# Weight pieces prepared only in the up stages, stored at once from six buffers; sums of the first down projection taken earlier, seven operand pairs

## The chip, the cores and the metric

The kernel runs on one core of one Trainium2 chip. The metric is device time in microseconds (us), the median of three runs. A core has TensorE (PE, matrix products), ScalarE (ACT), VectorE (DVE), GpSimd (POOL) and SyncE (SP). SP computes nothing; it issues transfers. POOL here issues the stores of activations.

## The reference

Attention in two steps through 32 packed queries, a gated MLP, and a second MLP with h·cos(h):

```python
p_packed = sm_attn(p, k, v)                 # 8 batches, 8 heads, 576 tokens, head size 64
out = sm_attn(q, p_packed, p_packed)
x = out.transpose(0, 2, 1, 3).reshape(4608, 512)
g = x @ w_gate                              # 512 -> 1536
x = (g / (1 + exp(-g)) * (x @ w_val)) @ w_out     # 1536 -> 512
h = x @ w_in                                # 512 -> 2048
out = (h * cos(h)) @ w_out2                 # 2048 -> 512
```

The weights arrive as 64-bit floats.

## The kernel before

Products are made in three passes of two-part operands: each operand is split into a high part (ACT copies it with rounding) and a low part (DVE subtracts), and PE multiplies high by high, high by low, low by high. That is the helper `split` (lines 85 to 87).

The work has three stages, one after the other on PE.

*Up stages, one for each batch 0 to 7* (`a_up`, lines 429 to 479). A batch has 24 slots: 12 column blocks f of the gated MLP, two token halves c. In a slot PE makes two groups of six matmuls of 288 columns (`pg` and `pv`, line 462), ACT takes the silu of the one (line 470), DVE multiplies by the other (line 471), and after the second half POOL stores the pair to DRAM as `h1` (line 478). A table `sched` hangs further steps on the end of a slot: the scores of later batches, loads of keys, queries and values, and `w2_step`. Batch 0 makes its weights with `a_wp0` (lines 400 to 412), later batches with `a_wp`.

*First down projection* (loop at lines 770 to 806, product in `strassen`, line 549). The tokens are taken in five sets, four with 512 columns to a product and one with 256. Each set is a two-by-two scheme with seven products, in the order 0, 4, 6, 1, 3, 2, 5. A product is 36 matmuls in two halves m. `prep` splits the operands of the next product, three pairs `g` to a product; for products 1 and 5 it first makes differences of the loaded activations `hr` (lines 519 to 523). The weights of the seven products are in `w1u`, the results go to `x2d`.

*Second MLP* (lines 819 to 980), fed from `w2u` and `w2d` in DRAM.

What links the stages is the preparation of weights. 88 pieces of 128x256 are loaded as 64-bit words (`raw`), decoded by two ACT and two DVE operations (`w2t`, `w2f`, lines 97 to 110), for the first 56 pieces combined into Strassen sums (`w2c`, line 346), split (`w2p`) and stored to `w1u` (42 stores), `w2u` (56) and `w2d` (32, for the last 32 pieces, which need no sums). `w2_step` (lines 387 to 396) does this in halves: an even step stores what is ready, loads the piece two ahead, does up to two pending splits and decodes one piece; an odd step does one pending split. There are 16 steps in each of batches 1 to 6, 24 in batch 7, and 56 in the first four sets of the down projection, two to a product.

The order on each engine is the order of the code. Engines wait for each other by semaphores, and an engine that waits holds up all that is behind it. SP has one queue, in which loads and stores follow each other.

Of the kernel before, what the change touches and what calls it, by code (L numbers as in the profile page):

```python
# [10 lines left out]
F32 = mybir.dt.float32  # L11
# [21 lines left out]
NG = NPF // 2  # L33
ATT = 26
ORDER = (0, 4, 6, 1, 3, 2, 5)
# [9 lines left out]
def attention_mlp_kernel(ctx: ExitStack, tc: tile.TileContext, qT, kT, vP, pP, wgv, w12, out):  # L45
# [4 lines left out]
    st = ctx.enter_context(tc.tile_pool(name="st", bufs=4))  # L50
    stage = {n: ExitStack() for n in ("dc", "ups", "att", "gates", "da", "db", "dw")}

# [3 lines left out]

    dc, att = pool("dc"), pool("att")
    gw, ups = pool("gates", "right"), pool("ups", "right")
# [262 lines left out]

    w2_raw, w2_f, w2_todo, w2_done = {}, {}, [], []
    NITEM = 2 * NW1 + 4 * NF2

    def w2_load(i):
        if i < NITEM:
            r = w2_raw[i] = dc.tile([128, 256, 2], U32, tag="r", name="raw", bufs=3)
            SP.dma_start(
                out=r, in_=w12[i // 2, :, 256 * (i % 2):256 * (i % 2) + 256].bitcast(U32).rearrange(
                    "p (n t) -> p n t", t=2)  # L330
            )

    def w2_small(name):
        return dc.tile([128, 256], F32, tag="s", name=name, bufs=10)
# [44 lines left out]

    def w2_store():  # L380
        while w2_done:
            p, dst = w2_done.pop(0)
            SP.dma_start(out=dst, in_=p.bitcast(F32))

    w2_n = [0]

    def w2_step():
        s_ = w2_n[0]
        w2_n[0] += 1
        if s_ % 2 == 0 and s_ // 2 < NITEM:  # L390
            w2_store()
# [36 lines left out]

    def a_up(b, sched):
        def side(k):  # L430
# [3 lines left out]
        for f in range(NF1):  # L434
# [8 lines left out]
            if b == 0:  # L443
                for u in range(2):
                    for c in range(2):
                        for o, p_ in zip((0, 128), banks[c]):
                            PE.matmul(
                                out=p_, lhsT=w[:, u, o:o + 128], rhs=a2[0, u][:, HS * c:HS * c + HS],
                                start=(u == 0), stop=(u == 1),
                            )  # L450
                    if u == (f == 0) and f + 1 < NF1:
                        a_wp0(f + 1)
            for c in range(2):
                sl = slice(HS * c, HS * c + HS)
                pg, pv = banks[c]
                for o, p_ in ((0, pg), (128, pv)):
                    n = 0
                    for u in range(2):
                        if b == 0:
                            continue  # L460
                        for (x, y) in PASSES:
                            PE.matmul(  # L462
                                out=p_, lhsT=w[u][:, x, o:o + 128], rhs=a2[b, u][:, y, sl],
                                start=(n == 0), stop=(n == 5),
                            )
                            n += 1
                if b == 0 and f > 0:
                    u_step(2, 1)
                s_ = ups.tile([128, HS], F32, tag="silu", name="silu", bufs=4)
                ACT.activation(out=s_, in_=pg, func=AF.Silu)  # L470
                DVE.tensor_tensor(out=h_[:, sl], in0=s_, in1=pv, op=ALU.mult)  # L471
                if b == 0:
                    u_step(0, 1)
                    u_step(1, 1)
                    if f == 0:
                        u_step(2, 1)
                if c == 1:
                    nc.gpsimd.dma_start(out=h1[f, :, S * b:S * b + S], in_=h_)
                side(2 * f + c)

# [25 lines left out]
    def new_g(N):  # L506
        n = g_n[0] % 5
        g_n[0] += 1
        return late["da" if n < 2 else "db"].tile(
            [128, 2, 2, N], F32R, tag="g", name="g", bufs=2 if n < 2 else 3  # L510
        )

    def prep(s_, n, fp):
        if s_ >= len(SETS):
            return
        N = SETS[s_][1]
        x11, x21, x22, x12 = (raw1.get((s_, k, t, fp)) for k, t in ((0, 0), (1, 0), (1, 1), (0, 1)))
# [6 lines left out]
        src = {0: x11, 4: x21, 6: x22, 1: x22, 3: x11, 2: x12, 5: x21}[n]  # L524
        g = g1[n, fp] = new_g(N)
        split(src, g[:, 0], g[:, 1])

# [102 lines left out]
    with tc.manual_schedule():  # L630
# [87 lines left out]
        for b in range(B):  # L718
# [14 lines left out]
            else:  # L733
# [18 lines left out]
            a_up(b, sched)  # L752
            w2_store()

# [12 lines left out]
        def nxt(s_, i):  # L767
            return (s_, ORDER[i + 1]) if i < 6 else (s_ + 1, ORDER[0])

        for s_ in range(len(SETS)):  # L770
            end = s_ == len(SETS) - 1
            for i in range(7):
                evict0 = strassen(s_, i, 0)
                if not end:
                    w2_step()
                prep(*nxt(s_, i), 0)
# [3 lines left out]
                prep(*nxt(s_, i), 2)  # L780
                if i == 3:
                    load_h(s_ + 1, 0, 0)
                elif i == 4:
                    load_h(s_ + 1, 1, 0)
                elif i == 5:
                    load_h(s_ + 1, 1, 1)
                    load_h(s_ + 1, 0, 1)
                if not end:
                    w2_step()
                elif i == 4:  # L790
                    w2_store()
# [4 lines left out]
                elif i == 5:  # L796
# [4 lines left out]
                elif i == 6:  # L801
                    sums_x2(2)
# [4 lines left out]

        for n in ("db", "da", "dc"):
            stage[n].close()
# [211 lines left out]
```

## Time and profile before

| | us |
|---|---|
| median of 3 runs (lowest, highest) | 1645.67 (1644.96, 1646.34) |
| the profiled execution | 1643.67 |
| its span in the profile | 1641.8 |
| PE busy in it | 1508.0 (92%) |
| DVE busy, ACT busy | 1123.9 (68%), 866.2 (53%) |
| mean granted TensorE clock | 0.961 of full |

The span starts with the first instruction and ends with the last; 1.9 us of the profiled execution lie around it. PE is busy for 92% on average, but the second of the page's views, which cuts the span in 40 slices, shows nine tenths or more in each of the last 18 and less in most of those before. The three stages therefore have to be read apart.

### The profile page before, as it was taken

The numbers are of one execution on the slowest core, as the hardware profiler recorded it, in microseconds if no ns is written. First come the engines' busy times: TensorE is split into PE (matmuls) and PEld (weight loads), VectorE is DVE, ScalarE is ACT, GpSimd is POOL, SyncE is SP. The second block draws the span as 40 slices with busy tenths as digits, with TensorE's granted clock in tenths as the row PEclk, the third lists the DMA queues.
The fourth block names the chain that finished last, engine by engine and source line by source line (L and its number), as shares of the span: only waits on it lengthen the run. The fifth ranks groups of instructions, "written<-read, shape, count | busy, mean of one in ns | idle before, by whom it ended". The sixth has DMA issues, their size and how long they took to land.

```text
span 1641.8 us, 26374 instructions
## 1 busy us (share of the span) xinstructions
PE 1508.0 (92%) x9432; PEld 1287.0 (78%) x9432; DVE 1123.9 (68%) x2139; ACT 866.2 (53%) x1847; POOL 76.6 (5%) x158
## 2 busy tenths in 40 slices
PE   9898888889978588988888999999999999999999
PEld 6567777777867366767767899999999999999997
DVE  6756776777856377666768777677667667667564
ACT  5755645646645144534535655655656556555552
POOL 0001111111110000001000000000000000000000
PEclk9989999999989788989889999999999999999999
DMA  9926557655488744635615866656666666666641
GB/s 339 331 95 224 204 186 250 210 186 209 166 280 288 287 124 171 202 129 174 219 59 209 321 190 223 205 201 227 198 215 209 202 218 200 217 204 202 194 145 64
DMA packets 160626, 335.72 MB, mean 204 GB/s; under 512 B 16880, under 2 KB 35312, under 8 KB 160496
## 3 DMA queue, kind: packets, MB, share of 16 engines
q1 hardware_dynamic: 149872, 296.28, 54.0%
q0 software_dynamic: 10624, 37.76, 5.9%
q8 instruction: 75, 1.23, 0.3%
q14 instruction: 55, 0.45, 0.1%
HBM read 252.71 MB, written 81.26 MB: 203 GB/s over the span
## 4 chain that ended last, share of the span: by engine, by line
PE 52%; DVE 7%; DMA 4%; ACT 3%; issue 2%; SPq 0%; ACTq 0%; DVEq 0%
PE acc L884 24%; PE p L869 21%; PE o L549 7%; ACT g L86 2%; DMA raw<-in_w 1%; DMA w<-w1u 1%; DVE g L87 1%; DVE hr L520 1%; DVE hr L521 1%; DVE hr L519 1%; DVE hr L523 1%; DMA w2d<-w2p 1%; DVE x2e L569 0%; DMA hr<-h 0%; DVE xs L87 0%
## 5 line engine op out<-in xcount | busy, mean ns | idle before, releaser
L884 PE MATMUL acc<-wd,g 128*128 128x512 f32 x1728 | 418.1, 391 | 0.0
L869 PE MATMUL p<-xs,up 128*128 128x384 f32 x2016 | 379.2, 339 | 2.1 <-DMA up<-w2u 1.4
L884 PEld LDWEIGHTS acc<-wd,g 128*128 128x128 f32 x1728 | 323.0, 188 | 61.4
L869 PEld LDWEIGHTS p<-xs,up 128*128 128x128 f32 x2016 | 359.0, 188 | 14.0 <-DMA up<-w2u 1.4
L549 PE MATMUL o<-g,w 128*128 128x512 f32 (+1 forms) x1260 | 294.4, 393 | 65.3 <-ACT g L86 45.3
L549 PEld LDWEIGHTS o<-g,w 128*128 128x128 f32 x1260 | 232.2, 201 | 127.2 <-ACT g L86 52.0
L462 PE MATMUL pg<-a,wp 128*128 128x288 f32 x1008 | 173.5, 309 | 36.7 <-ACT silu L470 28.2
L462 PEld LDWEIGHTS pg<-a,wp 128*128 128x128 f32 x1008 | 148.3, 196 | 60.9 <-ACT silu L470 30.3
L847 ACT ACTIVATE t<-c,quarter 128x384 f32<-128x384 f32 x144 | 88.6, 615 | 201.1 <-DVE c L957 195.3
L462 PE MATMUL pv<-a,wp 128*128 128x288 f32 x1008 | 167.1, 302 | 4.8 <-DVE h L471 3.0
L86 ACT ACTIVATE g<-hr 128x1024 fp32r<-128x1024 f32 (+1 forms) x105 | 98.8, 966 | 136.2 <-DVE hr L521 74.4
L87 DVE TENSOR_TENSOR g<-hr,g 128x1024 fp32r<-128x1024 f32 (+1 forms) x105 | 115.0, 1116 | 68.4 <-ACT g L86 67.9
L462 PEld LDWEIGHTS pv<-a,wp 128*128 128x128 f32 x1008 | 147.8, 194 | 7.6 <-DVE h L471 4.4
L471 DVE TENSOR_TENSOR h<-silu,pv 128x288 f32<-128x288 f32 x192 | 85.8, 447 | 51.5 <-PE pv L462 21.0
L470 ACT ACTIVATE silu<-pg 128x288 f32<-128x288 f32 x192 | 76.8, 410 | 67.2 <-PE pg L462 57.3
L857 DVE TENSOR_TENSOR g<-t,g 128x384 fp32r<-128x384 f32 x192 | 105.9, 551 | 8.0 <-ACT g L844 7.8
L952 DVE TENSOR_TENSOR u<-v,p 128x384 f32<-128x384 f32 x48 | 26.6, 554 | 119.4 <-PE p L869 119.0
L849 DVE TENSOR_TENSOR t<-t,k 128x384 f32<-128x384 f32 x192 | 106.0, 552 | 3.1 <-ACT k L853 1.5
L850 ACT ACTIVATE t<-t 128x384 f32<-128x384 f32 x192 | 98.1, 511 | 2.5 <-DVE t L849 2.4
L844 ACT ACTIVATE g<-t 128x384 fp32r<-128x384 f32 x192 | 98.7, 514 | 0.4 <-DVE t L855 0.4
L853 ACT ACTIVATE k<-t 128x384 int32<-128x384 f32 x192 | 98.1, 511 | 0.0
L898 DVE TENSOR_TENSOR oacc<-oacc,acc 128x512 f32<-128x512 f32 x108 | 73.8, 684 | 34.6 <-PE acc L884 34.6
(100 smaller groups left out, 1509.0 us busy)
## 6 DMA issues: line engine op xcount, KB each, us to landing
up<-w2u SPq DMA_DIRECT2D x336, 256.0 KB, 3.1
wd<-w2d SPq DMA_DIRECT2D x96, 512.0 KB, 6.2
h<-h POOLq DMA_DIRECT2D x96, 288.0 KB, 3.2
hr<-h SPq DMA_DIRECT2D x48, 512.0 KB, 7.2
raw<-in_w SPq DMA_DIRECT2D x88, 256.0 KB, 3.6
w2u<-w2p SPq DMA_DIRECT2D x56, 256.0 KB, 2.6
raw<-in_wgv SPq DMA_DIRECT2D x24, 512.0 KB, 8.6
w1u<-w2p SPq DMA_DIRECT2D x42, 256.0 KB, 2.4
```

The lines of the kernel that those rows point to most:

```text
L86: ACT.activation(out=hi, in_=src, func=AF.Copy)
L87: eng.tensor_tensor(out=lo, in0=src, in1=hi.bitcast(F32), op=ALU.subtract)
L462: PE.matmul(out=p_, lhsT=w[u][:, x, o:o + 128], rhs=a2[b, u][:, y, sl], start=(n == 0), stop=(n == 5),)
L549: PE.matmul(out=acc, lhsT=wd1[n, fp][:, j, 256 * x + 128 * m:256 * x + 128 * m + 128], rhs=g1[n, fp][:, y, j, :], start=(first and q == 0) ...
L844: ACT.activation(out=three["g"][:, 0, :], in_=three["t"], func=AF.Copy)
L847: ACT.activation(out=now["t"], in_=now["h"], func=AF.Identity, scale=1.0 / TWO_PI, bias=quarter)
L849: DVE.tensor_tensor(out=one_["t"], in0=one_["t"], in1=one_["k"], op=ALU.subtract)
L850: ACT.activation(out=one_["t"], in_=one_["t"], func=AF.Sin, scale=SIN_SCALE)
L853: ACT.activation(out=now["k"], in_=now["t"], func=AF.Copy)
L857: DVE.tensor_tensor(out=three["g"][:, 1, :], in0=three["t"], in1=three["g"][:, 0, :].bitcast(F32), op=ALU.subtract)
L869: PE.matmul(out=out, lhsT=w[:, u, 128 * k:128 * k + 128], rhs=x[:, v, k, :], start=(first and k == 0 and i == 0), stop=(last and k == 1 an ...
L884: PE.matmul(out=acc, lhsT=gs[p, a, t][:, x, o:o + 128], rhs=wd[j, f][:, y, :], start=(f == 0 and n == 0), stop=(f == 3 and n == 2),)
```

## The change

`w2_step` now hangs on 22 of the 24 slots of batches 1 to 6 (all but 1 and 6) and twice on every slot of batch 7; none is left in the down projection. A split piece is stored by SP in the same step, where it was collected and stored at the next even step, and the split pieces have six buffers instead of three. The buffers lie in the pool of the up stages, which closes before the down projection; the attention pool has 24 buffers instead of 26. In batch 0 the weights of blocks 3 and 9 are made one block earlier.

In the down projection the differences leave `prep` for a table by product, `sums1`, which stands ahead of the splits; there are seven operand pairs instead of five, the loads for the next set are put at the products with numbers 4 and 5 in the order, and ten small matmuls (`keep_busy(10)`) stand ahead of the first product.

```diff
-ATT = 26
+ATT = 24
 def w2_put(w_, dst):
     def go():
-        p = dc.tile([128, 2, 256], F32R, tag="p", name="w2p", bufs=3)
+        p = ups.tile([128, 2, 256], F32R, tag="p", name="w2p", bufs=6)
         split(w_, p[:, 0, :], p[:, 1, :])
-        w2_done.append((p, dst))
+        SP.dma_start(out=dst, in_=p.bitcast(F32))
...
+        def packed(f):
+            if f < NF1 and f not in ahead:
+                ahead.add(f)
+                a_wp0(f)
...
+                    if f in early:
+                        packed(f + 2)
...
-        n = g_n[0] % 5
+        n = g_n[0] % 7
...
-        if n == 1:
-            DVE.tensor_tensor(out=x11, in0=x12, in1=x11, op=ALU.subtract)
-            DVE.tensor_tensor(out=x12, in0=x22, in1=x12, op=ALU.subtract)
-            DVE.tensor_tensor(out=x22, in0=x22, in1=x11, op=ALU.subtract)
-        elif n == 5:
-            DVE.tensor_tensor(out=x21, in0=x21, in1=x22, op=ALU.subtract)
+    def sums1(s_, i):
+        todo = {
+            0: [((0, 1), (0, 1), (0, 0), fp) for fp in range(3)],
+            2: [((1, 1), (1, 1), (0, 1), fp) for fp in range(3)],
+            3: [((0, 0), (1, 1), (0, 0), fp) for fp in range(3)],
+            4: [((1, 0), (1, 0), (1, 1), 0)],
+            5: [((1, 0), (1, 0), (1, 1), fp) for fp in (1, 2)],
+        }
+        for to, x, y, fp in todo.get(i, ()):
+            to, x, y = (raw1[s_, k, t, fp] for k, t in (to, x, y))
+            DVE.tensor_tensor(out=to, in0=x, in1=y, op=ALU.subtract)
...
-                    for k in (4, 7, 8, 9, 10, 11, 12, 13, 15, 16, 17, 18, 19, 21, 22, 23):
-                        put(sched, k, w2_step)
+                    for k in range(24):
+                        if k not in (1, 6):
+                            put(sched, k, w2_step)
                 else:
                     for k in range(24):
-                        put(sched, k, w2_step)
+                        put(sched, k, w2_step, w2_step)
...
+        keep_busy(10)
         for s_ in range(len(SETS)):
             for i in range(7):
                 evict0 = strassen(s_, i, 0)
-                if not end:
-                    w2_step()
+                sums1(s_, i)
                 prep(*nxt(s_, i), 0)
                 prep(*nxt(s_, i), 1)
                 evict0()
                 evict1 = strassen(s_, i, 1)
                 prep(*nxt(s_, i), 2)
...
-                if not end:
-                    w2_step()
```

How the order on the engines moves is shown at three places.

ACT in batch 7, from the middle of the batch: `w2t` and `w2f` are the two decode operations of a piece, `w2p` the high part of its split, `silu` the activation of a slot. Before:

```order
L98 ACTIVATE w2t<-raw 128x256
L99 ACTIVATE w2f<-raw,low_90 128x256
L470 ACTIVATE silu<-pg 128x288 x2
L86 ACTIVATE w2p<-w2c 128x256 x2
L98 ACTIVATE w2t<-raw 128x256
```

Now:

```order
L98 ACTIVATE w2t<-raw 128x256
L99 ACTIVATE w2f<-raw,low_87 128x256
L86 ACTIVATE w2p<-w2f 128x256
L471 ACTIVATE silu<-pg 128x288
L98 ACTIVATE w2t<-raw 128x256
```

A piece was spread over two slots, and two silus stood between its decoding and its split; now each slot has a whole piece, and the split, which needs DVE's part of the decoding, follows the decoding with nothing between.

DVE at the start of the down projection, set 0, product 0 and what follows (`hr` are loaded activations, `g` the low parts of the operand pairs, `x2e` a result; the numbers tell the buffers apart). Before, from the splits for the second product on:

```order
L87 TENSOR_TENSOR g_7153<-hr_6580,g_7153 128x1024
L87 TENSOR_TENSOR g_7156<-hr_6582,g_7156 128x1024
L87 TENSOR_TENSOR g_7180<-hr_6584,g_7180 128x1024
...
L108 SCALAR_TENSOR_TENSOR w2f_7275<-raw_7145,w2f_7275 128x256
L519 TENSOR_TENSOR hr_6376<-hr_7096,hr_6376 128x1024
L520 TENSOR_TENSOR hr_7096<-hr_6586,hr_7096 128x1024
L521 TENSOR_TENSOR hr_6586<-hr_6586,hr_6376 128x1024
L87 TENSOR_TENSOR g_7284<-hr_6586,g_7284 128x1024
```

Now:

```order
L87 TENSOR_TENSOR g_7410<-hr_6652,g_7410 128x1024
L534 TENSOR_TENSOR hr_7425<-hr_7425,hr_6648 128x1024
L534 TENSOR_TENSOR hr_7427<-hr_7427,hr_6650 128x1024
L534 TENSOR_TENSOR hr_7429<-hr_7429,hr_6652 128x1024
L87 TENSOR_TENSOR g_7488<-hr_6872,g_7488 128x1024
L87 TENSOR_TENSOR g_7491<-hr_6874,g_7491 128x1024
L87 TENSOR_TENSOR g_7515<-hr_6876,g_7515 128x1024
```

Three differences that stood two products later, one chain of three to a pair and behind a decoding, now stand ahead of the splits for the second product; they read the third quarter of the activations, `hr_7425` to `hr_7429`.

SP at the same place: the load of that quarter, behind the weights of the second and third products. DMASW are the semaphores of POOL's stores, DMAHW those of SP's own transfers. Before:

```order
L489 DMA w_7094<-w1u 128x2x512 [waits DMAHW5_49,PE_49]
L502 DMA hr<-h_79 128x2x512 [waits DMAHW6_49,PE_49]
L502 DMA hr<-h_79 128x2x512 [waits DMAHW7_49,PE_49]
L502 DMA hr<-h_79 128x2x512 [waits DMAHW0_49,DMASW1_49,DMASW0_49]
L489 DMA w_7102<-w1u 128x2x512 [waits DMAHW1_49]
```

Now:

```order
L492 DMA w_7423<-w1u 128x2x512 [waits DMAHW3_49,PE_49]
L505 DMA hr<-h_76 128x2x512 [waits DMASW6_49,DMASW4_49,DMAHW4_49,DMASW2_49,DMASW0_49]
L505 DMA hr<-h_76 128x2x512 [waits DMASW5_49,DMASW6_49,DMASW3_49,DMASW7_49,DMASW1_49,DMAHW5_49,DMASW0_49,DVE_49]
L505 DMA hr<-h_76 128x2x512 [waits DMAHW6_49,DMASW5_49]
L492 DMA w_7431<-w1u 128x2x512 [waits DMAHW7_49,PE_49]
```

The buffers of this quarter now lie over those from which POOL stores the last activations, and SP waits for those stores at this point.

## Rows read from the trace of the kernel before

**Rows 1.** Windows: busy us (instructions) of each engine, granted clock, DMA share, GB/s

```profile
295.80:356.80 61.00, 53.30 (x537) 45.07 (x522) 43.85 (x106) 33.79 (x86) 6.75 (x14) 0.94 0.62 215
356.80:413.20 56.40, 53.48 (x578) 44.49 (x578) 44.07 (x107) 33.57 (x86) 6.75 (x14) 1.00 0.53 188
...
464.80:522.60 57.80, 44.25 (x329) 40.69 (x327) 33.10 (x82) 27.07 (x73) 5.98 (x11) 0.85 0.85 303
...
551.40:882.00 330.60, 267.49 (x1152) 212.32 (x1153) 224.85 (x279) 134.81 (x208) 20.10 (x37) 0.88 0.46 154
```

**Rows 2.** Waits of PE from 522 to 884 us: total, times, longest

```profile
PE o L549 <- ACT g L86: 45.3, 14, 18.3
PE o L549 <- DVE x2e L569: 10.0, 5, 2.8
PE o L549 <- DVE g L87: 7.8, 17, 0.8
```

**Rows 3.** Timeline of PE, down projection: start, us, count, [idle before, releaser]

```profile
522.59 2.06 PE L549 MATMUL o<-g,w 128*128 128x512 f32 x7
...
528.70 22.67 PE L549 MATMUL o<-g,w 128*128 128x512 f32 x95 [0.76 <-DVE g L87]
...
787.49 13.60 PE L549 MATMUL o<-g,w 128*128 128x256 f32 x96 [1.36 <-ACT g L86]
...
877.98 4.36 PE L549 MATMUL o<-g,w 128*128 128x512 f32 x18 [2.77 <-DVE x2e L569]
882.18 2.99 PE L869 MATMUL p<-xs,up 128*128 128x384 f32 x16
```

**Rows 4.** Chain that ended last, 518 to 890 us: start, us, what

```profile
552.96 10.01 DMA raw<-in_w
```

**Rows 5.** Timeline from 223 to 230 us, ACT, DVE and PE

```profile
226.03 0.42 ACT L86 ACTIVATE w2p<-w2c 128x256 fp32r<-128x256 f32 x1 [8.14 <-DMA w1u<-w2p]
...
227.17 0.41 ACT L98 ACTIVATE w2t<-raw 128x256 f32<-128x256 f32 x1
...
227.49 0.51 ACT L99 ACTIVATE w2f<-raw,low 128x256 int32<-128x256 uint8 x1
227.90 0.39 ACT L470 ACTIVATE silu<-pg 128x288 f32<-128x288 f32 x1
228.03 0.42 DVE L105 SCALAR_TENSOR_TENSOR w2f<-w2t,w2f 128x256 uint32<-128x256 uint32 x1 [0.30 <-ACT w2f L99]
...
228.34 1.81 PE L462 MATMUL pg<-a,wp 128*128 128x288 f32 x6 [5.50 <-ACT silu L470]
228.49 0.42 DVE L108 SCALAR_TENSOR_TENSOR w2f<-raw,w2f 128x256 uint32<-128x256 uint32 x1
```

**Rows 6.** Groups by line and form: busy us, mean ns, idle before

```profile
L87 DVE TENSOR_TENSOR g<-hr,g 128x1024 fp32r<-128x1024 f32 x84 | 101.0, 1222 | 62.6 <-ACT g L86 62.2
...
L87 DVE TENSOR_TENSOR w2p<-w2c,w2p 128x256 fp32r<-128x256 f32 x56 | 22.1, 414 | 52.5 <-ACT w2p L86 52.5
...
L521 DVE TENSOR_TENSOR hr<-hr 128x1024 f32<-128x1024 f32 x12 | 14.7, 1225 | 0.5
```

**Rows 7.** DMA issues: KB each, median us from issue to landing

```profile
h<-h POOLq DMA_DIRECT2D x96, 288.0 KB, 3.2
hr<-h SPq DMA_DIRECT2D x48, 512.0 KB, 7.2
```

**Rows 8.** Timeline of PE, batch 0

```profile
81.91 1.58 PE L404 MATMUL wp<-wg,ppT 64*32 64x256 f32 x16 [3.52 <-ACT E L179]
```

**Rows 9.** Timeline of PE, batch 7, after a wait and later

```profile
505.73 1.64 PE L462 MATMUL pg<-a,wp 128*128 128x288 f32 x6
507.17 1.26 PE L462 MATMUL pv<-a,wp 128*128 128x288 f32 x6
508.27 0.96 PE L462 MATMUL pg<-a,wp 128*128 128x288 f32 x6
509.07 0.96 PE L462 MATMUL pv<-a,wp 128*128 128x288 f32 x6
```

More of the change, by code (lines that the diff above doesn't have):

```diff
@@ L50, in attention_mlp_kernel @@
     st = ctx.enter_context(tc.tile_pool(name="st", bufs=4))
-    stage = {n: ExitStack() for n in ("dc", "ups", "att", "gates", "da", "db", "dw")}
+    stage = {n: ExitStack() for n in ("ups", "att", "gates", "da", "db", "dw")}
     def pool(n, side=None):
@@ L55, in pool @@
         return stage[n].enter_context(tc.tile_pool(name=n, bufs=1, reuse_waits="tile", **kw))
-    dc, att = pool("dc"), pool("att")
+    att = pool("att")
     gw, ups = pool("gates", "right"), pool("ups", "right")
@@ L320, in u_step @@
             u_next[k] += 1
-    w2_raw, w2_f, w2_todo, w2_done = {}, {}, [], []
+    w2_raw, w2_f, w2_todo = {}, {}, []
     NITEM = 2 * NW1 + 4 * NF2
@@ L326, in w2_load @@
         if i < NITEM:
-            r = w2_raw[i] = dc.tile([128, 256, 2], U32, tag="r", name="raw", bufs=3)
+            r = w2_raw[i] = ups.tile([128, 256, 2], U32, tag="r", name="raw", bufs=3)
             SP.dma_start(
@@ L378, in w2_work @@
                 w2_todo.pop(0)()
[L380 to L383, printed above, removed]
     w2_n = [0]
@@ L390, in w2_step @@
         if s_ % 2 == 0 and s_ // 2 < NITEM:
-            w2_store()
             w2_load(s_ // 2 + 2)
@@ L427, in a_wp, with a_up @@
             split(p, wp[b, m, r][:, 0], wp[b, m, r][:, 1])
-    def a_up(b, sched):
+    def a_up(b, sched, early=()):
+        ahead = {0}
+        def packed(f):
+            if f < NF1 and f not in ahead:
+                ahead.add(f)
+                a_wp0(f)
         def side(k):
@@ L450, in a_up @@
                             )
-                    if u == (f == 0) and f + 1 < NF1:
-                        a_wp0(f + 1)
+                    if u == (f == 0):
+                        packed(f + 1)
             for c in range(2):
@@ L506, in new_g @@
     def new_g(N):
-        n = g_n[0] % 5
+        n = g_n[0] % 7
         g_n[0] += 1
         return late["da" if n < 2 else "db"].tile(
-            [128, 2, 2, N], F32R, tag="g", name="g", bufs=2 if n < 2 else 3
+            [128, 2, 2, N], F32R, tag="g", name="g", bufs=2 if n < 2 else 5
         )
@@ L516, in prep @@
         N = SETS[s_][1]
-        x11, x21, x22, x12 = (raw1.get((s_, k, t, fp)) for k, t in ((0, 0), (1, 0), (1, 1), (0, 1)))
-        if n == 1:
-            DVE.tensor_tensor(out=x11, in0=x12, in1=x11, op=ALU.subtract)
-            DVE.tensor_tensor(out=x12, in0=x22, in1=x12, op=ALU.subtract)
-            DVE.tensor_tensor(out=x22, in0=x22, in1=x11, op=ALU.subtract)
-        elif n == 5:
-            DVE.tensor_tensor(out=x21, in0=x21, in1=x22, op=ALU.subtract)
-        src = {0: x11, 4: x21, 6: x22, 1: x22, 3: x11, 2: x12, 5: x21}[n]
-        g = g1[n, fp] = new_g(N)
-        split(src, g[:, 0], g[:, 1])
+        k, t = {0: (0, 0), 4: (1, 0), 6: (1, 1), 1: (1, 1), 3: (0, 1), 2: (0, 0), 5: (1, 0)}[n]
+        g = g1[n, fp] = new_g(N)
+        split(raw1[s_, k, t, fp], g[:, 0], g[:, 1])
+    def sums1(s_, i):
[9 more added lines that the diff above has]
+            DVE.tensor_tensor(out=to, in0=x, in1=y, op=ALU.subtract)
     acc1, part = {}, {}
@@ L751, in attention_mlp_kernel @@
                 late["da"] = pool("da")
-            a_up(b, sched)
-            w2_store()
+            a_up(b, sched, (1, 7) if b == 0 else ())
         stage["ups"].close()
@@ L780, in attention_mlp_kernel @@
                 prep(*nxt(s_, i), 2)
-                if i == 3:
+                if i == 4:
                     load_h(s_ + 1, 0, 0)
-                elif i == 4:
+                    load_h(s_ + 1, 0, 1)
+                elif i == 5:
                     load_h(s_ + 1, 1, 0)
-                elif i == 5:
                     load_h(s_ + 1, 1, 1)
-                    load_h(s_ + 1, 0, 1)
-                if not end:
-                    w2_step()
-                elif i == 4:
-                    w2_store()
+                if end and i == 4:
                     load_x2(0)
@@ L795, in attention_mlp_kernel @@
                     x_now = [new_xs() for _ in range(7)]
-                elif i == 5:
+                elif end and i == 5:
                     sums_x2(0)
@@ L800, in attention_mlp_kernel @@
                     split_x2(3, x_now)
-                elif i == 6:
+                elif end and i == 6:
                     sums_x2(2)
@@ L806, in attention_mlp_kernel @@
                 evict1()
-        for n in ("db", "da", "dc"):
+        for n in ("db", "da"):
             stage[n].close()
```

2 lines of the change are left out of this document (1 added, 1 removed).

## The prediction

> **What bounds the kernel now.** I read the page's slices first, then the windows by stage, then what PE waits for in the weak stage, then single stretches of the timeline. The second MLP, from 882.18 us on, keeps PE full and is not touched. The first down projection runs on PE from 522.59 to 882.18, that is 359.6 us [rows 3]. Its floor comes from its undisturbed stretches: 95 matmuls in 22.67 us are 0.2386 each, 96 of the narrow ones in 13.60 us are 0.1417 [rows 3]; 4 sets x 252 x 0.2386 + 252 x 0.1417 = 276.2 us. So 83.4 us are lost here. Three waits make 63.1 of them, 45.3 for ACT's high parts `g` [rows 2]; the other 20 are matmuls at a granted clock that averages 0.88 [rows 1]. What holds ACT up is seen in the chain: a load of a 64-bit piece, 10.01 us behind the weights on SP's queue [rows 4], for the longest wait of 18.3 us [rows 2]; and DVE's chains of three differences, 1.225 each [rows 6], made in the product before they are needed.
>
> The up stages are nearly full on PE, 53.3 us of 61.0 in batch 4 and 53.48 of 56.4 in batch 5 [rows 1], which does the same work but loads no values for a later batch. The 4.6 us between them are one stall: ACT waits 8.14 us for a `w2p` buffer that a store has not left, and PE idles 5.50 us behind it [rows 5]. Batch 7 takes 57.8 us for 44.25 of PE, at clock 0.85 [rows 1].
>
> **The change part by part.**
>
> *No preparation in the down projection.* 28 of the 88 pieces go from here. With them go the load behind the weights and the decodings between splits. What ACT and DVE keep for a product of 36 x 0.2386 = 8.6 us: at most three differences and three splits of 1.22 each and, as an estimate by its half size, an eviction of 0.6 on DVE: 3 x 1.225 + 3 x 1.222 + 0.6 = 7.9 us [rows 6]. It fits in products 0, 2 and 3 of the order with 0.7 to spare, in the others with several. The seventh pair lets the third split of a product begin without waiting for PE to leave a pair. So I cost waits in the running sets at nothing; if that cover is thin and each of the three heavy products slips 1 us in four sets, it is 12 us.
>
> *The start of this stage.* Here the new order has a wait. The three differences at product 0 stand on DVE ahead of the splits for the second product and need the third quarter of the activations. SP issues its loads only when POOL's last stores have landed. The last multiply of batch 7 comes, by my estimate, some 4 us after PE's first product begins, because DVE still has that batch's last piece and a split ahead of it; the store lands 3.2 us after its issue and the loads 7.2 us after theirs [rows 7], which with POOL's issue is about 15 us; then 3 x 1.225 of differences and a split of 1.222 [rows 6]: 20 us after the start. The first product ends after about 11 (8.6, and 2.5 of waiting for its own late splits). PE waits 9 to 10 us. Queued behind DVE's wait are all splits of product 2 and behind those PE; behind SP's are twelve weight loads, needed three products later. At best the loads are quick and nothing waits (0), at worst they queue behind 3 MB of weights for the next two products, 10 us more.
>
> *Sum of the stage.* 276.2 + 2.5 + 10 of waits + 2.8 at the end, where the loads for the second MLP stay as they are [rows 3], + the clock after waits, taken as before at 20/63 of them, 4.9: 296 us. That is 63 us less. With the bounds: 75 less (no wait at the start) to 41 less (10 later, 12 in the running sets).
>
> *Batches 1 to 6.* Each takes 11 pieces instead of 8. A heavy piece costs DVE two decodings of 0.42 [rows 5], 1.75 splits and one difference of about 0.414 each [rows 6], 2.0 us, so three add 6 us: 44.07 becomes 50 in batch 5, of 56.4 us [rows 1]. ACT goes from 33.6 to about 39. PE's 53.5 stay the longest, and hide it; if DVE's waits in its own order do not shrink, a batch grows by some of the 6. I take 1 us a batch. Six buffers hold three splits more, at seven splits in eight slots of 2.3 us some 8 us, which is the wait they meet: the 4.6 go in batches 1 to 4. Together 4 x (1 - 4.6) + 1 = -13 us. Batch 6 has light pieces now (two decodings and a split, 1.26), 11 x 1.26 against 8 x 2.0: 0. Bounds: -18 (all added work hidden) to +12 (5 us in five batches, 13 won).
>
> *Batch 7.* 22 light pieces in 22 slots, and in each slot the split follows its own decoding: ACT and DVE wait for each other in turn. Rows 5 give the round: from `w2t` at 227.17 to the end of the second DVE part at 228.91 it is 1.74; then the high part and the silu, with about 0.05, 0.33 and 0.30 to the next `w2t`: 2.4 us. PE's part of a slot is two groups at 0.80, 1.6 us [rows 9]. So ACT and DVE set the pace: 20 x 2.4 + two extra weight splits of 2 us each + 4 until the first pair of the next stage is ready = 56. Two bursts of 3 MB (activations and weights for the next stage) stand ahead of pieces loaded only two slots ahead; at 303 GB/s [rows 1] each takes 10 us and may hold ACT 5 us, of which I take 3. That gives 62 against 57.8: +4. Loads and stores of this batch come to 21.4 MB (22 pieces and 22 stores of 0.26, 9 + 3 transfers of 0.52, 12 stores of 0.29). The window moved 303 GB/s at a share of 0.85 [rows 1], so 356 full: 60 us, about the same. Bounds -3 (bursts hidden and the old waits gone) to +14 (70 us, all at 303).
>
> *Batch 0.* Making blocks 3 and 9 earlier takes up to 3.52 us of waiting at the ninth block [rows 8]; -3, between -6 and +2 (two attention buffers fewer). Everything else in it stands as before.
>
> *Sum.* -63 - 13 + 4 - 3 = -75. The profiled execution took 1643.7 us, 1.9 of them outside the span; the median of the runs is 2.0 above it. 1643.7 - 75 + 2.0 = 1570.7; **1571 us**.
>
> **A rule weighed.** PE's clock after waits is seen in batch 7: after one of 5 us two groups start 1.44 us apart, a little later 0.80 [rows 9]. In the down projection waits of under 1 us left the pace at 0.2386 [rows 3]. The Trainium skill, in "TensorE: Matmul & The Clock Gate", section "A second HAM failure mode: psum-queue depth-cycling", says that PE idling briefly and often between matmul groups, as it cycles through PSUM banks, makes the clock swing between its levels. The rows so far do not show that for gaps under 1 us.
>
> **The rivals.**
>
> *The clock falls in batch 7.* PE will idle about 0.8 us in each slot, waiting for banks. At the lower level a slot takes 2 x 1.44 = 2.9 us and PE sets the pace: 24 x 2.9 + 4 = 74 instead of 62: 1583 us. By the rule above this is what happens. For it: nothing but the gaps; against it, the gap of 0.76 us followed by full pace [rows 3].
>
> *Nothing waits at the start, and the added work is all hidden.* 12 less in the down stage with its clock, 5 in batches 1 to 5, 7 in batch 7: 1547. For it: DVE idles 12 us in batch 5 [rows 1], and the third quarter might be asked for earlier than I think. Against: the wait for POOL's stores is in the order.
>
> *The loads were the cause.* The removal of the pieces only uncovers the loads of activations, 7.2 us each three [rows 7], at set boundaries: 8 us x 4 = 32 more than forecast, 1603. For it: six such loads now follow each other where the steps between them spread them. Against: they are issued one and a half products, some 13 us, ahead.
>
> *Slower: the clock stays low through the up stages.* If the denser order on ACT and DVE leaves PE gaps in every slot of batches 1 to 7 and the clock goes to 1.2 GHz, each batch costs 24 x 2 x 0.64 = 31 us more. It outweighs 75 us from two and a half batches on; with all seven it is +217, some 1790. Against it: batch 5 ran at clock 1.00 with DVE busy 78% [rows 1].
>
> **How the numbers follow.** Forecast as worked out 0.62; the clock in batch 7 0.08; all hidden 0.13; the loads 0.07, and with it a worse start of the stage by 20 us (1591) 0.07; slower 0.03. The likeliest one's own range is 1555 to 1587. The range of 8 in 10 leaves out most of the loads, the slower case and the far end of the hidden one: 1548 to 1602. Runs of this kernel differ by 0.1%, so 0.2%, about 3 us, is what can be told: within it lies only the near edge of the slower case, 0.02; faster 0.95, slower 0.03.
>
> **What would show it.** Right: the down projection takes about 296 us from its first matmul to its last, with one wait of about 10 us at the second product and nearly none from there to the end of the stage; batches 1 to 4 last 56 to 58 us and no wait of ACT for a `w2p` buffer over 2 us is left; batch 7 lasts about 62 us with ACT's `w2t` 2.4 us apart. Wrong: waits for `hr` at later sets (the loads), two groups 1.44 us apart through most of batch 7 (the clock), no wait at product 2 (hidden), or a second MLP that differs by more than 3 us from its 760 us.

## The result, and the profile after

The changed kernel takes 1559.17 us (median of 4 runs, 1558.54 to 1561.92) against 1645.32 us; the ratio is 0.9479, with an interval of 0.9462 to 0.9495. The profiled execution took 1558.54 us, with a span of 1556.7 us. The forecast was 1571 us, with a range of 1548 to 1602.

By stages, with two kernels of the experiments that the rest needs: e8 is the kernel before with the new sums alone, e12 is e8 with six buffers (a batch goes from its predecessor's last `h` store to its own, batch 7 to the first matmul of the down projection, this to the first matmul of the second MLP; us of the profiled execution):

| stage | before | after | predicted | e8 | e12 |
|---|---|---|---|---|---|
| batch 0 | 112.2 | 108.4 | -3 | 113.6 | 110.4 |
| batches 1 to 6 | 352.6 | 325.4 | -13 | 355.0 | 320.1 |
| batch 7 | 57.8 | 78.3 | +4 | 57.3 | 47.7 |
| down projection | 359.6 | 283.7 | -63 | 286.2 | 285.4 |
| second MLP | 759.6 | 760.9 | 0 | 760.3 | 763.8 |

First the windows of batch 4, batch 5, batch 7 and the running sets of the down projection, with the columns of [rows 1].

```profile
278.00:331.40 53.40, 49.91 (x533) 42.12 (x531) 48.01 (x121) 37.65 (x98) 6.73 (x15) 1.00 0.82 287
331.40:386.60 55.20, 51.28 (x546) 43.38 (x540) 48.68 (x122) 37.60 (x98) 6.74 (x15) 1.00 0.67 230
433.80:512.10 78.30, 49.82 (x356) 43.62 (x354) 39.45 (x94) 35.69 (x93) 5.95 (x11) 0.83 0.80 265
541.80:795.80 254.00, 249.29 (x1202) 208.08 (x1201) 192.49 (x204) 107.14 (x131) 21.64 (x40) 1.00 0.40 141
```

Batch 4 is now as short as batch 5, with DVE 4 us busier than in [rows 1]; batch 7 has become the weak stage, and the running sets of the down projection have a granted clock of 1.00 where it was 0.88. Its waits of PE answer to [rows 2]: 45.3, 10.0 and 7.8 us have become these.

```profile
PE o L557 <- DVE g L87: 10.5, 3, 8.9
PE p L873 <- DMA up<-w2u: 4.7, 1, 4.7
PE o L557 <- ACT g L86: 1.7, 2, 1.2
```

The timeline of PE through batch 7 and the down projection answers to [rows 3, 9].

```profile
455.29 1.81 PE L463 MATMUL pg<-a,wp 128*128 128x288 f32 x6 [11.88 <-DVE wp L87]
...
458.33 1.64 PE L463 MATMUL pg<-a,wp 128*128 128x288 f32 x6
459.77 1.06 PE L463 MATMUL pv<-a,wp 128*128 128x288 f32 x6
460.67 0.96 PE L463 MATMUL pg<-a,wp 128*128 128x288 f32 x6
461.47 0.95 PE L463 MATMUL pv<-a,wp 128*128 128x288 f32 x6
...
482.29 1.81 PE L463 MATMUL pg<-a,wp 128*128 128x288 f32 x6 [12.02 <-ACT silu L471]
...
498.95 1.05 PE L463 MATMUL pg<-a,wp 128*128 128x288 f32 x6 [0.55 <-ACT silu L471]
...
501.36 1.06 PE L463 MATMUL pg<-a,wp 128*128 128x288 f32 x6 [0.57 <-ACT silu L471]
...
517.14 8.73 PE L557 MATMUL o<-g,w 128*128 128x512 f32 x30 [0.76 <-DVE g L87]
534.81 256.28 PE L557 MATMUL o<-g,w 128*128 128x512 f32 x1223 [8.94 <-DVE g L87]
795.80 21.92 PE L873 MATMUL p<-xs,up 128*128 128x384 f32 x108 [4.71 <-DMA up<-w2u]
```

There is one wait of 8.94 us at the second product; then PE works for 256 us without one. What the 8.94 us wait for is seen on DVE (start, us, count): the first differences wait for the loads of the third quarter.

```profile
529.71 3.91 DVE L534 TENSOR_TENSOR hr<-hr 128x1024 f32<-128x1024 f32 x3 [10.76 <-DMA hr<-h]
533.54 5.76 DVE L87 TENSOR_TENSOR g<-hr,g 128x1024 fp32r<-128x1024 f32 x5
```

In batch 7 the two waits of 12 us stand behind ACT, which waits for a raw piece.

```profile
451.81 0.43 ACT L98 ACTIVATE w2t<-raw 128x256 f32<-128x256 f32 x1 [10.33 <-DMA raw<-in_w]
...
479.73 0.43 ACT L98 ACTIVATE w2t<-raw 128x256 f32<-128x256 f32 x1 [11.13 <-DMA raw<-in_w]
...
498.80 0.43 ACT L98 ACTIVATE w2t<-raw 128x256 f32<-128x256 f32 x1
...
501.21 0.42 ACT L98 ACTIVATE w2t<-raw 128x256 f32<-128x256 f32 x1
```

SP's queue shows what stands ahead of the first of these two pieces: six loads of 0.5 MB each.

```profile
437.01 1.68 SPq L505 DMA_DIRECT2D hr<-h  x3
438.78 2.61 SPq L492 DMA_DIRECT2D w<-w1u  x3
441.43 1.48 SPq L328 DMA_DIRECT2D raw<-in_w  x1
```

SP begins to hand over the six loads at 437.01 and comes to the piece only at 441.43.

### The profile page after: what moved, and what is told of

It is laid out like the page before. It is cut to its first block, busy times and chain, and to the rows that moved or that the text cites. A ratio compares the mean times of both kernels' runs of the same rounds, so it can differ in the third digit from the quotient of the medians.

```text
span 1556.7 us, 26541 instructions
## 1 busy us (share of the span) xinstructions
PE 1475.7 (95%) x9452; PEld 1271.4 (82%) x9452; DVE 1117.6 (72%) x2139; ACT 866.0 (56%) x1847; POOL 76.3 (5%) x158
## 3 DMA queue, kind: packets, MB, share of 16 engines
q1 hardware_dynamic: 149872, 296.28, 56.9%
## 4 chain that ended last, share of the span: by engine, by line
PE 65%; issue 26%; POOL 3%; DVE 2%; ACT 2%; DMA 1%; POOLq 0%; SPq 0%; DVEq 0%; ACTq 0%
PE acc L888 25%; PE p L873 22%; PE o L557 16%; POOL h L479 3%; DMA hr<-h 0%; DMA raw<-in_wgv 0%; PE wm L115 0%; DMA h<-h 0%; PE pg L448 0%; PE pv L448 0%; DVE wg L105 0%; DVE xs L87 0%; ACT k L857 0%; ACT t L851 0%; ACT E L179 0%
## 5 line engine op out<-in xcount | busy, mean ns | idle before, releaser
L557 PE MATMUL o<-g,w 128*128 128x512 f32 (+1 forms) x1260 | 267.4, 374 | 12.2 <-DVE g L87 10.5
L557 PEld LDWEIGHTS o<-g,w 128*128 128x128 f32 x1260 | 221.4, 190 | 57.9 <-DVE g L87 11.9
L463 PE MATMUL pg<-a,wp 128*128 128x288 f32 x1008 | 169.9, 304 | 28.6 <-ACT silu L471 14.9
L463 PEld LDWEIGHTS pg<-a,wp 128*128 128x128 f32 x1008 | 144.2, 191 | 54.1 <-ACT silu L471 20.0
L463 PE MATMUL pv<-a,wp 128*128 128x288 f32 x1008 | 163.9, 298 | 5.3 <-DVE h L472 4.3
L463 PEld LDWEIGHTS pv<-a,wp 128*128 128x128 f32 x1008 | 144.4, 190 | 8.5 <-DVE h L472 7.0
```

The source lines that it names most:

```text
L463: PE.matmul(out=p_, lhsT=w[u][:, x, o:o + 128], rhs=a2[b, u][:, y, sl], start=(n == 0), stop=(n == 5),)
L557: PE.matmul(out=acc, lhsT=wd1[n, fp][:, j, 256 * x + 128 * m:256 * x + 128 * m + 128], rhs=g1[n, fp][:, y, j, :], start=(first and q == 0) ...
```

## The experiments

Each is an edit of the changed kernel, e8 and e12 of the kernel before.

**e1, three buffers.**

```diff
-            p = ups.tile([128, 2, 256], F32R, tag="p", name="w2p", bufs=6)
+            p = ups.tile([128, 2, 256], F32R, tag="p", name="w2p", bufs=3)
```

> The changed kernel with three w2p buffers instead of six; pieces are still stored at once. Theory (the six buffers take away the wait for a store behind the value loads): ACT waits 5 to 9 us for a w2p buffer again in batches 1 to 4 and PE idles 4 to 6 us behind each, so those four batches grow by 18 to 24 us together over the changed kernel's, and the whole by about as much (1577 to 1583 us). Rival (storing at once already frees the buffers early enough, the six are not needed): no such wait, within 3 us of the changed kernel, 1556 to 1562.

Measured: 1573.67 us (1569.27 to 1575.67), 14.5 above the changed kernel; batches 1 to 6 take 338.4 us instead of 325.4. The waits of ACT from 109 to 348 us (total, times, longest) have the buffers' stores in them again, which the changed kernel has none of:

```profile
ACT w2p L86 <- DMA w2u<-w2p: 15.9, 6, 8.1
ACT w2p L86 <- DMA w1u<-w2p: 12.3, 7, 5.1
```

The mechanism is the theory's; the price is 13 us instead of 18 to 24. Batches 1, 3 and 4 grow by 3.3, 2.0 and 8.6 us, the others by less than 1 or not at all.

**e2, late sums.**

```diff
+        if n == 1:
+            DVE.tensor_tensor(out=x11, in0=x12, in1=x11, op=ALU.subtract)
+            DVE.tensor_tensor(out=x12, in0=x22, in1=x12, op=ALU.subtract)
+            DVE.tensor_tensor(out=x22, in0=x22, in1=x11, op=ALU.subtract)
...
-                sums1(s_, i)
...
-                if i == 4:
+                if i == 3:
```

> The changed kernel with the differences made again one product before they are needed, among the splits (three at once for product 1, one for product 5 of a set), and the loads of activations at their old places; the seven pairs stay and no preparation of weights returns. Theory (the earlier differences are a gain of their own): waits of PE for ACT's g of 2 to 4 us at one or two products in each of five sets, with a slower clock behind them, less the wait of 9 us at the second product of the stage, which goes: the down projection takes 8 to 20 us more than 283.7, in all 1567 to 1579. Rival (only the pieces that were removed made ACT and DVE late): the down projection within 4 us of 283.7, or shorter by the wait at its start, 1550 to 1562.

Measured: 1608.53 us (1608.34 to 1610.38), 49 above the changed kernel; the down projection takes 333.6 us. The theory had the sign, at less than half the size, and the rival is out. DVE's timeline shows why it costs so much:

```profile
536.05 1.22 DVE L522 TENSOR_TENSOR hr<-hr 128x1024 f32<-128x1024 f32 x1
537.30 1.23 DVE L523 TENSOR_TENSOR hr<-hr 128x1024 f32<-128x1024 f32 x1
538.56 1.23 DVE L524 TENSOR_TENSOR hr<-hr 128x1024 f32<-128x1024 f32 x1
540.97 1.23 DVE L87 TENSOR_TENSOR g<-hr,g 128x1024 fp32r<-128x1024 f32 x1 [1.19 <-ACT g L86]
542.11 1.22 DVE L522 TENSOR_TENSOR hr<-hr 128x1024 f32<-128x1024 f32 x1
```

Every split is three differences, then a wait of 1.2 us for ACT's high part, then the low part: 6.1 us, three times in a row, for a product of 36 x 0.2312 = 8.3 us. With the differences made earlier DVE does five splits in 5.76 us (its row after the change, above). DVE's work is the same, 213 us in this stage against 209; it is the order that makes PE late. ACT's waits in the stage (513.17 to 846.8 us) say the same; the largest is for the last of the three differences:

```profile
ACT g L86 <- DVE hr L524: 88.6, 15, 9.4
```

The edit also puts the loads of activations back at their old places. That is not what costs: ACT waits 0.3 us for such a load in the whole stage, and DVE never. What PE then pays is half waiting and half clock. The window of the whole stage in e2:

```profile
513.17:846.80 333.63, 291.31 (x1261) 231.98 (x1261) 213.45 (x222) 117.47 (x147) 22.80 (x42) 0.92 0.40 136
```

The same stage in the changed kernel:

```profile
512.07:795.80 283.73, 267.41 (x1260) 221.43 (x1261) 208.75 (x222) 117.89 (x147) 22.72 (x42) 0.97 0.46 161
```

The same 1260 matmuls are busy for 291.3 us and 267.4, 24 of the 50 us.

**e3, five pairs.**

```diff
-        n = g_n[0] % 7
+        n = g_n[0] % 5
...
-            [128, 2, 2, N], F32R, tag="g", name="g", bufs=2 if n < 2 else 5
+            [128, 2, 2, N], F32R, tag="g", name="g", bufs=2 if n < 2 else 3
```

> The changed kernel with five operand pairs instead of seven; the sums stay early. Theory (the forecast's: the seventh pair is what lets the third split of a product start without waiting for PE): the heavy products 0, 2 and 3 each slip by about 1 us in four sets, so the down projection takes 5 to 15 us more than 283.7, in all 1564 to 1575. Rival (the sums alone give ACT and DVE enough room): within 3 us, 1556 to 1562.

Measured: 1559.44 us (1557.24 to 1561.32), the down projection 284.3: no difference. The rival is right.

**e4, the old down projection without its pieces**: the edits of e2 and e3 together.

> The changed kernel with the old down projection in all but the preparation of weights: late differences, old places of the loads, five pairs. It tells how much of the stage's 75.9 us the removed pieces give by themselves. Theory (the pieces and their load behind the weights were the larger part): the down projection takes 300 to 315 us, between 283.7 and the 359.6 of before, in all 1575 to 1590. Rival (sums and pairs give most of it, the pieces little): over 320 us, 1597 and more. Second rival (pieces alone give all): under 290, 1556 to 1565.

Measured: 1607.68 us (1606.24 to 1609.35), the down projection 334.2. That is where the first rival put it: taking the pieces out of the old order gives 25 of the 75.9 us.

**e5, first sums one product later.**

```diff
-            0: [((0, 1), (0, 1), (0, 0), fp) for fp in range(3)],
+            (1 if s_ == 0 else 0): [((0, 1), (0, 1), (0, 0), fp) for fp in range(3)],
```

> The changed kernel with the three differences of the first set's product 0 moved to its product 1; the other sets as they are. Theory (DVE waits for the third quarter of the activations with the splits for product 2 queued behind it): the wait of 8.94 us at the second product goes, and with it the slow matmuls behind it, 8 to 11 us less, 1548 to 1551 us. Rival (something else, the splits' own data or the weights, is late there as well): a wait of 5 to 9 us at the second or third product stays and the time is within 4 us of the changed kernel.

Measured: 1549.77 us (1547.78 to 1551.08), the down projection 273.4 instead of 283.7, as the theory has it. PE's timeline from the second product on:

```profile
534.76 246.27 PE L557 MATMUL o<-g,w 128*128 128x512 f32 x1187 [0.15 <-DVE g L87]
```

**e6, the loads of batch 7 one by one.**

```diff
-                    put(sched, 0, lambda: load_h(0, 0, 0), lambda: load_w1(0))
-                    put(sched, 6, lambda: load_h(0, 1, 0), lambda: load_h(0, 1, 1))
+                    for fp in range(3):
+                        put(sched, 2 * fp, lambda fp=fp: load_h(0, 0, 0, (fp,)))
+                        put(sched, 6 + 2 * fp, lambda fp=fp: load_w1(0, (fp,)))
+                        put(sched, 12 + 2 * fp, lambda fp=fp: load_h(0, 1, 0, (fp,)))
+                        put(sched, 18 + 2 * fp, lambda fp=fp: load_h(0, 1, 1, (fp,)))
```

> The changed kernel with the two bursts of six loads in batch 7 (activations and weights for the down projection) spread as single loads of 0.5 MB over slots 0 to 22 of that batch. Theory (each burst of 3 MB holds the next raw piece back by 10 us, with ACT and then PE behind it): the two waits of ACT of 10.3 and 11.1 us shrink to under 2 us and PE's 11.9 and 12.0 go; batch 7 takes 60 to 64 us instead of 78.3; in all 1541 to 1546 us. Rival (the batch is held by the bytes it moves, whatever their order): the waits come back in smaller parts, batch 7 stays over 72 us, the time within 6 us of the changed kernel.

Measured: 1553.79 us (1553.51 to 1554.37), batch 7 70.7 us. That is nearer to the rival, which had over 72 us in the batch: PE's waits of 11.9 and 12.0 come back in parts.

```profile
450.42 1.81 PE L463 MATMUL pg<-a,wp 128*128 128x288 f32 x6 [5.58 <-DVE wp L87]
...
477.06 1.36 PE L463 MATMUL pg<-a,wp 128*128 128x288 f32 x6 [4.28 <-DVE wp L87]
```

ACT still waits 14.3 us for raw pieces, in seven parts of at most 4.0. The batch moved 276 GB/s at a DMA share of 0.86; e11 below shows 364 GB/s in it, so the queue was not full all the time here. Our reading, which no run tests by itself, is that a raw piece asked for two slots ahead comes late behind a single load of 0.5 MB too.

**e7, splits a slot behind their decoding.**

```diff
-                        if k not in (1, 6):
+                        if k not in (1, 6) or (b == B - 2 and k == 1):
```

> The changed kernel with one more step of the preparation in batch 6, so that in batch 7 each split stands one slot behind the decoding of its piece. Theory (in batch 7 ACT and DVE wait for each other in every slot, as the split follows its own decoding): the round of 2.41 us between two w2t falls to 1.7 to 2.0, the batch outside its two long waits gets 8 to 14 us shorter, in all 1545 to 1552 us. Rival (the engines' work itself sets the round): 2.3 to 2.4 us again, within 3 us of the changed kernel.

Measured: 1556.58 us (1553.83 to 1557.95), batch 7 77.2 us: the rival's time, for neither's reason. ACT's timeline has a shorter round, 2.11 us from one `w2t` to the next where nothing else stands between. ACT's waits for DVE's decoding fall from 20.5 to 13.6 us in the batch, and its waits for raw pieces, which take the place of what was won, rise from 22.1 to 27.2:

```profile
483.58 0.42 ACT L98 ACTIVATE w2t<-raw 128x256 f32<-128x256 f32 x1
...
485.69 0.42 ACT L98 ACTIVATE w2t<-raw 128x256 f32<-128x256 f32 x1
...
503.14 0.43 ACT L98 ACTIVATE w2t<-raw 128x256 f32<-128x256 f32 x1 [1.86 <-DMA raw<-in_w]
```

**e8, the new sums alone**, in the kernel before.

```diff
+    def sums1(s_, i):
...
                 if not end:
                     w2_step()
+                sums1(s_, i)
...
-                if i == 3:
+                if i == 4:
                     load_h(s_ + 1, 0, 0)
+                    load_h(s_ + 1, 0, 1)
```

> The kernel before with the new sums (one to three products ahead) and the new places of the loads of activations alone: five pairs, 28 pieces still prepared in the down projection, stores and buffers of the up stages as before. Theory (the pieces cost by their load and by their work): the long wait of 18.3 us behind the weights stays or comes back elsewhere, and the down projection takes 325 to 350 us against 359.6, in all 1610 to 1637. Rival (late sums were the cause): under 310 us, 1596 or less.

Measured: 1572.34 us (1570.86 to 1574.29), ratio 0.9552 [0.9539, 0.9566]; the down projection takes 286.2 us with all 28 pieces in it. The theory falls. PE's timeline has the wait of the new order at the second product, and after the next product nearly none; the 18.3 us behind the weights are gone, though the piece stands in the queue where it stood.

```profile
549.34 19.98 PE L554 MATMUL o<-g,w 128*128 128x512 f32 x72 [11.94 <-DVE g L87]
571.05 177.11 PE L554 MATMUL o<-g,w 128*128 128x512 f32 x863 [1.73 <-DVE g L87]
```

ACT's waits in the stage show which of the two it was. Before (522 to 884 us) the largest was for the last of DVE's three differences:

```profile
ACT g L86 <- DVE hr L521: 74.4, 15, 6.7
```

In e8 (525 to 812 us) the waits for differences are these:

```profile
ACT g L86 <- DVE hr L531: 20.3, 10, 3.7
```

ACT's waits for raw pieces fall with them, from 34.1 us (the longest 21.5) to a single one of 5.7.

**e9, the edits of e5, e6 and e7 together.**

> The changed kernel with the edits of e5 (first sums one product later), e6 (single loads in batch 7) and e7 (splits a slot behind their decoding) together. If their gains add up: down projection 273 us as in e5, batch 7 6 to 8 us shorter as in e6 and e7, in all 1540 to 1544. If the bytes of batch 7, once the bursts are spread, are what is left to hold it, e7 adds nothing to e6 and the time is 1543 to 1546; if with the loads spread the round of 2.4 us is what holds it, e7 adds 3 to 6 us: 1536 to 1540.

Measured: 1542.09 us (1540.08 to 1543.78), batch 7 68.3 us. The three gains, 9.4, 5.4 and 2.6 us, add up to 1541.8. The second case, e7 adding nothing to e6, would be 1544.4 by the same numbers; it is 2.3 us off, and the runs spread over 3.7, so the two are not well told apart. The third is out.

**e10, half of batch 7's pieces in the down projection**, with e5's edit and five pairs.

```diff
-                        put(sched, k, w2_step, w2_step)
+                        put(sched, k, w2_step)
...
+                if s_ < 3 and i in (1, 4, 5, 6):
+                    w2_step()
                 evict1 = strassen(s_, i, 1)
                 prep(*nxt(s_, i), 2)
+                if s_ < 3 and i in (1, 4, 5, 6):
+                    w2_step()
```

> The changed kernel with e5's edit, five operand pairs, and half of batch 7's preparation (12 of its 24 pieces) done in the first three sets of the down projection, in products 1, 4, 5 and 6; the pieces' buffers stay open for it. Theory (in the down projection pieces cost next to nothing once the sums are early, as e8's 286.2 against 283.7 us says, while in batch 7 they cost some 20 us): batch 7 takes 56 to 60 us instead of 78.3, the down projection 273 to 277, in all 1528 to 1535. Rival (the forecast's: pieces in the down projection make ACT and DVE late): the down projection takes 285 us or more and eats half of the gain, 1540 or more.

Measured: 1517.63 us (1516.26 to 1519.48), below what the theory said: batch 7 takes 47.3 us, the down projection 269.9. Of the 22 pieces of batch 7 in the changed kernel 12 stay and 10 move. The bursts of 3 MB are unchanged; a piece is now loaded four slots ahead. ACT still waits 13.1 us for raw pieces, in four parts of at most 8.1, but PE's longest wait in the batch is

```profile
454.74 1.81 PE L463 MATMUL pg<-a,wp 128*128 128x288 f32 x6 [2.63 <-ACT silu L471]
```

**e11, e10 with e6's loads.**

> e10 with e6's edit too: the loads for the down projection one by one over batch 7. Theory (with half the pieces and no burst neither bytes nor the round of ACT and DVE hold batch 7, PE's own 44 to 48 us do): batch 7 takes 48 to 53 us, in all 1520 to 1527. Rival (the first pair for the down projection, or the loads, come late whatever their order): batch 7 stays over 55 us and the time within 3 us of e10.

Measured: 1511.62 us (1509.59 to 1512.95), ratio 0.9171 [0.9158, 0.9183]: the fastest, 47.5 us below the changed kernel. The windows of batch 7, from 0.7 us before its start, and of the down projection:

```profile
432.70:475.40 42.70, 42.70 (x361) 39.60 (x360) 31.49 (x71) 28.98 (x70) 6.49 (x12) 1.00 1.01 364
475.40:744.00 268.60, 264.52 (x1263) 220.33 (x1262) 213.82 (x242) 128.17 (x170) 21.62 (x40) 0.99 0.52 189
```

PE is full in batch 7, which is shorter than the theory's 48 to 53, and in the down projection 4.1 us without work are left. Spreading the loads gives 6 us here, as in e6.

**e12, six buffers**, in e8, with two attention buffers fewer.

```diff
-ATT = 26
+ATT = 24
...
-            p = dc.tile([128, 2, 256], F32R, tag="p", name="w2p", bufs=3)
+            p = dc.tile([128, 2, 256], F32R, tag="p", name="w2p", bufs=6)
```

> e8 (the kernel before with the new sums) with six w2p buffers instead of three and 24 attention buffers instead of 26; pieces and the late stores as before. Theory (the forecast's: six buffers alone cover the wait of ACT for a store behind the value loads): ACT's waits for a w2p buffer of 9 us go, batches 1 to 4 fall from 61.7, 63.0, 60.6 and 61.2 us to 56 to 58 each, in all 1550 to 1556. Rival (the stores, handed to the queue only two slots later, are what holds the buffers; storing at once is needed): batches 1 to 4 stay over 59 us each, in all 1565 to 1574.

Measured: 1529.18 us (1527.57 to 1531.32), ratio 0.9296 [0.9274, 0.9319]. The theory's mechanism holds and gives more than its price: batches 1 to 4 take 53.7, 54.1, 54.2 and 54.1 us, batch 5, which had no long stall, falls too (56.3 to 54.2), and batch 7 from 57.3 to 47.7. The stores are as late as before. ACT's waits from 112 to 356 us have no store in them:

```profile
ACT silu L470 <- PE pg L462: 50.9, 35, 2.5
...
ACT w2p L86 <- DVE w2c L346: 10.1, 8, 1.9
```

With this the change comes apart. The sums bring 1646.07 (the kernel before beside e8; 1644.6 to 1647.5 beside the others) to 1572.34 us, the six buffers 1572.34 to 1529.18; all the rest (28 pieces moved into the up stages, stores at once, seven pairs, two blocks made earlier, the small matmuls ahead of the stage) brings it back up to 1559.17. By the table of stages that rest is +30.6 in batch 7, +5.3 in batches 1 to 6, -1.7 in the down projection that it was to relieve, -2.0 in batch 0 and -2.9 in the second MLP. That the pieces in batch 7 are what costs is seen in e10, 32 us below e5: it moves 10 of them out, and its five pairs gave nothing in e3.

## Why the prediction was right, and what was wrong in it

The time lies 12 us below the forecast and in the range. Point by point:

**The start of the down projection: right.** Forecast were 9 to 10 us of waiting at the second product for differences behind the loads of the third quarter; 8.94 were measured, and e5, which takes the cause away, gives 10.3. Both ends of the wait came some 2.7 us later than forecast, so its length is nearer than its terms: the first product ended after 13.8 us instead of 11, the second began after 22.7 instead of 20.

**The floor: mis-sized by 13 us.** 276.2 us rested on two stretches right behind a wait [rows 3]. In the changed kernel the period of a set, between the same store of two sets (541.83 and 600.08), is 58.25 us, so 0.2312 a matmul and not 0.2386; the narrow set takes 29.84 us, 0.1184 a matmul and not 0.1417. That makes 4 x 58.25 + 29.84 = 262.8; 7.5 of the 13 us are the wide sets', 5.9 the narrow one's. The narrow stretch began at the lower clock, 0.50 of full; from 793.2 us on, at full clock, its matmuls are 0.119 apart.

```profile
787.49:790.50 3.01, 2.86 (x11) 2.57 (x12) 2.95 (x6) 2.42 (x6) 0.00 (x0) 0.50 0.26 85
```

The wide stretch had full clock from its start; the window below covers most of it.

```profile
530.00:551.00 21.00, 20.95 (x91) 16.58 (x89) 9.33 (x12) 6.58 (x11) 1.08 (x2) 1.00 1.04 375
```

Its 22.67 us hold a stall of about 0.3 near 534 us and the end of the last matmul; the 59 matmuls between 536.4 and 550.2 are 0.2342 apart. Why these are still 1.3% slower than in the running sets is open.

With the measured terms the forecast's sum closes: 262.8 + 3.2 at the first matmuls + 8.9 + 4.7 at the end + 4.6 of slower clock (267.4 busy less 262.8) = 284.2, against 283.7. The clock term was 4.9.

**"No preparation in the down projection": the step credited the wrong part.** It put the running sets' waits at nothing, which they are, and gave the removed pieces and their load as the first reason, the chains of differences as the second. With late sums the stage takes 359.6 with pieces and 334.2 without (e4); with early sums 286.2 (e8) and 284.3 (e3). So the sums are worth 73 us with the pieces in place and 50 without; the pieces 25 us in the old order and 2 in the new. The chain's 10 us load [rows 4] was not the cause by itself: in e8 it stands in the same place, and PE has no long wait behind it. The seventh pair, which the step counted on for its third split, is worth nothing (e3).

**Batches 1 to 6: the mechanism right, the stall too small.** 4.6 us was the difference of batch 4 and batch 5 [rows 1], and took batch 5 for undisturbed. Six buffers take 35 us from batches 1 to 6 (e8 to e12, 355.0 to 320.1): 7.6 a batch in 1 to 4, and batches 5 and 6 had 2.1 and 2.5 of it as well. Storing at once does part of the same work: e1, with three buffers but 18 pieces more in these batches, takes 338.4 where e8 takes 355.0. The other term, 1 us a batch for the three added pieces, is near in its sum and not in its parts: from e12 to the changed kernel batches 1 to 5 grow by 7.8 in all, and batch 6, with its light pieces, falls by 2.5. Together, against the kernel before, it is -27 where -13 was said; batches 1 to 4 take 56.9, 57.5, 55.2 and 53.4 us where 56 to 58 were said, and no wait for a buffer is left. Batch 0 gives 3.7 us instead of 3, but e12, which makes no block earlier, has 1.8 of it, so the forecast's reason is not shown to be the cause.

**Batch 7: mis-sized by 16 us.** The slot's round of 2.4 us came out at 2.41. Each burst was taken at 3 us of ACT's time, from a wait of 5 at most; it was 10.33 and 11.13. The step halved the lead of a piece, from four slots to two, and did not carry that into the bursts' price: SP takes 4.4 us to hand over the six loads, and the piece issued behind them at 441.43 is there at 451.8, 10.4 us later. Of these 14.8 us its lead of two slots, 4.8 us, covers a third. In e10, with a lead of four slots and half the pieces, the same bursts hold ACT 8.1 and 4.6 us and PE 2.6 at most; no run changes the lead alone. The other part is bytes. The batch moves 20.7 MB (265 GB/s over 78.3 us), and at e11's 364 GB/s, the most of any batch 7 here, that takes 57 us as an estimate; e12 moves 17.0. So by this estimate some 10 us come with the pieces, whatever their lead. The comparison with before hid the bursts, since there they held ACT too, at the buffers: 22.6 us for stores,

```profile
ACT w2p L86 <- DMA w2u<-w2p: 22.6, 4, 12.3
```

which six buffers take down to 14.5 (e12) with batch 7 at 47.7. So against before batch 7 lost 20.5 us where 4 was said, and against what the buffers alone would have given 30.6.

**The rivals.** The clock did not fall in batch 7 for the gaps: from 495 to 508 us, with PE waiting about 0.5 us in every slot, it stood at 1.00.

```profile
495.00:508.00 13.00, 10.50 (x70) 9.12 (x68) 8.71 (x22) 7.36 (x20) 1.63 (x3) 1.00 0.92 287
```

The Trainium skill's rule in "TensorE: Matmul & The Clock Gate", section "A second HAM failure mode: psum-queue depth-cycling", is not borne out by this row; the low clock of the batch, 0.83, stands in and behind its two long waits (groups 1.44 apart behind 455.29, 0.80 from 460.67 us on). Loads that wait at later sets, and a low clock in all up stages, did not come. "All hidden" was half so: more was won in batches 1 to 6, and the start of the down projection did wait.

That the total is as near as 12 us is in part luck, since errors cancel: 13 us at the floor and 14 in batches 1 to 6 too little won, 16 in batch 7 too little lost.

## What to carry to other kernels

When a change bundles several cures for one stage, price each alone: here the sums and the six buffers win 117 us, and the rest, above all the pieces moved into batch 7, costs 30 of them. Before work goes from a stage to another, look at the slack of both after the other cures; here the down projection had room for all 28 pieces as soon as DVE's chains stood one product earlier. A transfer's lead is counted in time, and doubling the steps in a slot halves it. For a floor, look at the granted clock inside the stretch, and leave out its stalls and its end: two stretches that looked undisturbed made it 13 us too high.

## What the runs showed of the hardware that was not expected

A raw piece of 256 KB takes 4.0 us from issue to landing as a median, and 10.4 us behind six loads of 0.5 MB (441.43 to 451.8 us); both are of the changed kernel.

```profile
raw<-in_w SPq DMA_DIRECT2D x88, 256.0 KB, 4.0
```

With loads, stores and PE all spread, batch 7 of e11 holds PE full at clock 1.00 while the DMA engines are at a share of 1.01 and 364 GB/s; its window stands with e11.
